# One table of single steps for the start, the weights and each pair of groups

## The chip, the cores and the metric

The kernel runs on one core of one Trainium2 chip. Its time is device microseconds of one execution. Three executions of the kernel before took 2050.55, 2051.13 and 2052.91 us, median 2051.13. The execution that was profiled took 2051.95 us, and its span, from the first instruction to the last, is 2050.2 us. Differences are stated against the median.

## The reference

Keys and values are one tensor: `kv` is averaged over 4 x 4 pixels and multiplied by `w_sr`. Every row of `q` attends to the 768 pooled keys of its batch. A maxout layer with three weight matrices and an output projection follows.

```python
kv_pool = kv.reshape(B, H // r, r, W // r, r, C).mean(axis=(2, 4))   # r = 4
kv_flat = kv_pool.reshape(B, -1, C) @ w_sr                           # 768 keys a batch
k = v = kv_flat
s = scale * (q @ k.transpose(0, 2, 1))
s = s - s.max(-1, keepdims=True)
a = np.exp(s)
a /= a.sum(-1, keepdims=True) + 1e-09
attn_out = a @ v
# then, for x = attn_out as rows of 128 columns
h = np.maximum(np.maximum(x @ w1, x @ w2), x @ w3)                   # 768 columns
return (h @ w_out).astype(np.float32)
```

There are 4 batches of 12288 queries with 128 columns. `q`, `kv` and `w_sr` come as 4-byte numbers, the four layer weights as 8-byte ones.

## The kernel before

The queries are cut into 96 groups of 512, 24 to a batch; a group has four tiles of 128 queries, and the hidden layer of a group six steps of 128 hidden columns. Nearly every operand is kept as two 2-byte halves, a high part and the rest, and a product is three matmuls: high by high, high by low, low by high. The steps of one group have one-letter names in the order tables:

- `S` (`scores`): six matmuls of 384 columns for one tile, into a PSUM tile of two banks; there are two such tiles. `m` (`soft_max`) takes the row maximum on DVE and makes the bias `nb`; `e` (`soft_exp`) is the exponential on ACT with its sum; `c` (`soft_hi`) casts to 2 bytes on ACT; `l` (`soft_lo`) subtracts on POOL and starts the DMA transpose into `aT` on SP's queue.
- `X` (`attend`): half of the attention's product for a group, nine matmuls of 512 columns into the one PSUM tile `ps_x`. `xh` (ACT) and `xl` (DVE) split the result.
- `H` (`hidden`): six matmuls into two PSUM tiles `ps_h`, for w2 − w1 and w3 − w1. `R` (ACT) is a relu of the first, `M` (DVE) a maximum with the second, `C` (ACT) the cast, `L` (POOL) the difference. The next `H` uses the same two PSUM tiles, so it needs `R` and `M` of this one.
- `O` (`project`): three matmuls into `ps_o`; the sixth of a group adds three for x times w1·w_out. `P` (DVE and a DMA transpose), `G` (DVE) and `T` (DVE, a store) turn, merge and scale the output.
- `qd`, `qc`, `qp`, `qh`, `ql`: load 1024 queries, multiply by column factors (POOL), take the size of each row (DVE maximum), split (ACT, DVE) and transpose by DMA.
- `k` (`keys_step`): pooling of the next batch's keys, twelve tiles of 512 KB, with adds on DVE and a few matmuls.

Every instruction on these engines is issued through `InOrder` (line 103 of the profile, a helper, which is why nearly all rows have one line): each engine works through its own instructions in program order. So a table's order is the order of each engine, and an instruction that waits holds back what stands behind it on its engine. SP's queue issues all DMAs in the same way, and a load waits until a buffer of its pool is free (`kv_piece` has 13, shared by key tiles and raw weights; `aT` 2; `q_sb` 2).

The order of the work has four sources. The first batch's keys and the first six tiles' softmax are written out by hand. The weights are a list `todo` of small steps, of which `more(n)` issues the next n at chosen places: `made` lists what one half of a weight matrix needs (clamp, shift, low bits, sign), `halves` and `splits` what follows. From then on `ORDER`, twelve rows for the twelve steps of two groups, is run 48 times by two nested loops; in it a token drains everything that waits for it. Exceptions for the first two groups (`FIRST`, `LEFT`, `ATTEND`, `OUTS`) and the last (`OUTS`, the lines after the loops) are coded separately. The key tiles of the next batch are loaded in `keys_step`, two a group in the groups 1 to 6 of a batch:

```python
if f in (1, 4) and 1 <= r <= 6:
    m = 2 * (r - 1) + f // 4
    n.load(m // R, m % R)
```

The raw 8-byte weights are turned into 4-byte numbers by integer steps on their two words (`Weights64`): the high word is cleared of its sign, clamped, shifted by three, given three bits of the low word and the sign. Then `rest` subtracts w1, `top` and `size_d` find a power of two for the scale, and `split_hi` and `split_lo` make the halves. `product_w1` computes w1·w_out.

At the end `last_project` computes the last group's output with queries as rows. It multiplies with both halves of the weights at once (256 columns), into separate columns of `ps_o` and `ps_x`, so that `last_finish` copies the low columns out on ACT and adds them on DVE before it scales.

Of the kernel before, what the change touches and what calls it, by code (L numbers as in the profile page):

```python
# [20 lines left out]
def kernel(  # L21
# [34 lines left out]
    R = 4  # L56
# [66 lines left out]
    def times(t, src, by, by2=None):  # L123
# [9 lines left out]
    col = const.tile([C, 1], F32, name="col")  # L133
    d_top = const.tile([P, 2, 4], F32, name="d_top")
# [15 lines left out]
    FIRST = (1, 1, 1, 1, 0, 1, 1, 1, 1, 2, 0, 1)  # L150
    LEFT = (12, 12, 12, 12, 12)
    LO_ON_DVE, HI_ON_DVE, HL_ON_DVE = ((), (6, 8), ())
    OUT_AT, OUT_ON = (1, 8), ("dve", "dve")
    ATTEND = {0: (4, 4), 1: (4, 4)}
    LATE = (1,)
    W_LOW, W_HIGH = 2.0 ** -15 * 1.125, 122879.9921875
    HB_ = 5
    ORDER = (
# [12 lines left out]
    )  # L171
    OUTS = {2: (), 3: (), 4: (0, 1, 2)}

    def sr_weights():
# [11 lines left out]
        times(col, ps[:, :1], 1.0)  # L186

# [16 lines left out]
    class Weights64:  # L204
# [7 lines left out]
        def __init__(self, n, w, h, hi, lo, wide=False):  # L212
            self.n, self.h, self.wide, self.w = n, h, wide, w
            self.lay = (lambda t: t.rearrange("p (t c) -> p t c", c=C)) if wide else lambda t: t
            self.hi, self.lo = hi, lo
# [16 lines left out]
        def shift(self):  # L232
            dve.tensor_scalar(
                out=self.e.bitcast(I32), in0=self.e.bitcast(I32), scalar1=3, scalar2=0x3FFFFFF8,
                op0=ALU.logical_shift_left, op1=ALU.bitwise_and,
            )
# [7 lines left out]
        def sign(self):  # L244
            dve.scalar_tensor_tensor(
                out=self.e.bitcast(I32), in0=self.r1, scalar=-0x40000000, in1=self.e.bitcast(I32),
# [6 lines left out]
        def rest(self, on=pool):  # L253
            on.tensor_tensor(out=self.e, in0=self.e, in1=W[0, self.h].e, op=ALU.subtract)
# [14 lines left out]
    def size_d(h):  # L269
        top = d_top[:, h]  # L270
        dve.tensor_reduce(out=top[:, 3:4], in_=top[:, :3], axis=AX.X, op=ALU.max)
        times(top[:, 3:4], top[:, 3:4], col)
        W["ps"] = spare(True)
        mm(out=W["ps"][:, :1], lhsT=ones, rhs=top[:, 3:4], start=True, stop=True)

    def sized_d(h):
        pow2(d_size[h], W.pop("ps")[:, :1], SMALL, LARGE)
# [46 lines left out]
    class Keys:  # L324


        def __init__(self, b):
# [3 lines left out]
            self.acc = {}  # L331
# [3 lines left out]
            self.top = tiny.tile([1, 1], F32, name="pool_top", bufs=2)  # L335
# [24 lines left out]
        def fold(self, s, i, n):  # L360

            view = self.pieces[s, i].rearrange("p (u j c) -> p u j c", u=KU, c=C)
            dve.tensor_tensor(out=view[:, :, :n], in0=view[:, :, :n], in1=view[:, :, n:2 * n], op=ALU.add)

        def gather(self, s, i, n, first, last):
# [4 lines left out]
            for u in range(KU):  # L370
# [13 lines left out]
        def gathered_size(self):  # L384
            self.turn_tops(True)
            self.tops()
            self.size(True)
            self.sized()

        def gathered_project(self, s):  # L390
            if s == 0:
                self.kps = (ps_x.tile([P, G], F32, name="ps_x"), ps_o.tile([P, NJ, C], F32, name="ps_o"))
            out = self.kps[1].rearrange("p j c -> p (j c)") if s == KS - 1 else self.kps[0][:, s * PW:]
# [5 lines left out]
        def gathered_hi(self, n):  # L399
            ps, ks = ((self.kps[0], slice(0, G)), (self.kps[1].rearrange("p j c -> p (j c)")[:, :PW], slice(G, NK)))[n]  # L400
            act.mul(out=self.k_hi[:, ks], in_=ps, mul=self.up)

        def gathered_lo(self, n):
            ps, ks = ((self.kps[0], slice(0, G)), (self.kps[1].rearrange("p j c -> p (j c)")[:, :PW], slice(G, NK)))[n]
# [26 lines left out]
        def turn_tops(self, first=False):  # L431
            self.tops_ps = spare(first)
            dve.tensor_reduce(out=self.m[:, KS:KS + 1], in_=self.m[:, :KS], axis=AX.X, op=ALU.max)
            mm(out=self.tops_ps[:1, :P], lhsT=self.m[:, KS:KS + 1], rhs=ident, start=True, stop=True)

        def tops(self):
            dve.tensor_reduce(out=self.top, in_=self.tops_ps[:1, :P], axis=AX.X, op=ALU.max)

        def size(self, first=False):
            self.size_ps = spare(first)  # L440
# [698 lines left out]
```

## Time and profile before

| | us |
|---|---|
| median of three runs | 2051.13 |
| the profiled execution's own time | 2051.95 |
| its span | 2050.2 |
| PE busy | 1981.4 (97%) |
| DVE busy | 1505.8 (73%) |
| ACT busy | 1453.6 (71%) |
| POOL busy | 1414.8 (69%) |
| mean granted TensorE clock | 0.988 |

Matmuls are pipelined, and their ends are modelled: a matmul of 512 columns is listed with 380 ns, though the next starts before that, so PE's busy time counts a small gap between two of them as busy. Where PE is dense, the distance between the starts is its real step. A stretch's busy time says more than that of the whole span, since the start and the end have other limits than the middle.

### The profile page before, as it was taken

What the parts mean: (1) busy time and instruction counts of PE and PEld (TensorE: products, weight loads), DVE (VectorE), ACT (ScalarE), POOL (GpSimd) and SP (SyncE); (2) the same over time, 40 slices, a digit from 0 to 9 for tenths busy, and PEclk for the clock granted to TensorE, in tenths of its full rate; (3) what the DMA queues carried; (4) which work ended last, traced back from release to release, by engine and by line L of the source; (5) the groups of instructions that cost most, each with busy time, mean ns of one, the idle gap of its engine ahead of it and who ended that gap; (6) DMA issues with size and microseconds to landing.
All of it is one profiled execution on the core that took longest, in us unless ns stands there. A gap on an engine that the chain in (4) does not pass through costs nothing.

```text
span 2050.2 us, 29146 instructions
## 1 busy us (share of the span) xinstructions
PE 1981.4 (97%) x9797; PEld 965.8 (47%) x9797; DVE 1505.8 (73%) x2471; ACT 1453.6 (71%) x2529; POOL 1414.8 (69%) x1068
## 2 busy tenths in 40 slices
PE   5599999999999999999999999999999999999998
PEld 4344444444444444444444444444444444444444
DVE  5758887777777887777777788677776777777775
ACT  3367777777777777777777777677777777777774
POOL 3357776777776677677777777777777777777764
PEclk8699999999999999999999999999999999999999
DMA  8268866767668866675667787666766665667662
GB/s 250 54 137 179 170 139 114 141 131 138 124 126 187 190 132 126 130 145 119 129 139 163 163 173 137 131 127 128 139 132 133 129 139 121 132 131 139 122 120 67
DMA packets 839960, 283.30 MB, mean 138 GB/s; under 512 B 813441, under 2 KB 814593, under 8 KB 839809
## 3 DMA queue, kind: packets, MB, share of 16 engines
q1 hardware_dynamic: 839808, 281.43, 67.2%
q8 instruction: 77, 1.26, 0.2%
q14 instruction: 75, 0.61, 0.1%
HBM read 53.54 MB, written 25.17 MB: 38 GB/s over the span
## 4 chain that ended last, share of the span: by engine, by line
PE 81%; DVE 7%; ACT 4%; DMA 4%; POOL 2%; issue 2%; SPq 0%; DVEq 0%; ACTq 0%; POOLq 0%
PE ps_h L103 31%; PE ps_o L103 18%; PE ps_x L103 17%; PE ps_s L103 15%; DMA aT<-ahl 3%; DVE h L103 1%; ACT ahl L103 1%; POOL ahl L103 1%; DVE w_e L103 1%; DVE q_row L103 1%; ACT a L103 1%; DVE mx L103 1%; ACT hh L103 1%; ACT xh L103 1%; DVE rs L103 1%
## 5 line engine op out<-in xcount | busy, mean ns | idle before, releaser
L103 POOL TENSOR_TENSOR ahl<-a,ahl 128x768 f16<-128x768 f32 x384 | 628.9, 1648 | 307.8 <-issue 188.1
L103 POOL TENSOR_TENSOR hl<-h,hh 128x512 f16<-128x512 f32 x575 | 670.4, 1176 | 191.8 <-ACT hh L103 191.4
L103 DVE SCALAR_TENSOR_TENSOR h<-ps_h,h 128x512 f32<-128x512 f32 x575 | 396.5, 690 | 185.8 <-ACT h L103 92.5
L103 ACT ACTIVATE h<-ps_h 128x512 f32<-128x512 f32 x575 | 341.7, 594 | 244.0 <-PE ps_h L103 240.5
L103 ACT CAST hh<-h 128x512 f16<-128x512 f32 x577 | 349.8, 615 | 170.1 <-DVE h L103 170.0
L103 DVE TENSOR_REDUCE mx<-ps_s 128x1 f32<-128x768 f32 x384 | 366.3, 954 | 108.6 <-PE ps_s L103 107.8
L103 PE MATMUL ps_h<-xh,d_hi 128*128 128x512 f16 x1150 | 437.3, 380 | 5.1 <-DVE h L103 2.7
L103 PE MATMUL ps_h<-xl,d_hi 128*128 128x512 f16 x1150 | 437.2, 380 | 2.9 <-DVE xl L103 2.9
L103 PE MATMUL ps_h<-xh,d_lo 128*128 128x512 f16 x1150 | 437.0, 380 | 0.0
L103 ACT ACTIVATE a<-ps_s,nb,q_sc 128x768 f32<-128x768 f32 x384 | 378.3, 987 | 66.5 <-DVE nb L103 60.4
L103 PE MATMUL ps_x<-aT,v_hi 128*128 128x512 f16 (+1 forms) x1188 | 376.4, 375 | 18.5 <-DMA aT<-ahl 16.7
L103 PE MATMUL ps_s<-k_hi,qT 128*128 128x384 f16 x1536 | 379.0, 329 | 10.6 <-ACT a L103 9.2
L103 PEld LDWEIGHTS <-d_hi 128*128 128x128 f16 x2308 | 226.3, 98 | 260.6 <-issue 6.5
L103 PE MATMUL ps_o<-hh,wo 128*128 128x512 f16 x1140 | 339.1, 379 | 0.0
L103 PEld LDWEIGHTS <-qT 128*128 128x128 f16 x2304 | 227.0, 99 | 203.6 <-issue 17.1
L103 ACT CAST ahl<-a 128x768 f16<-128x768 f32 x382 | 312.5, 832 | 4.5
L103 PEld LDWEIGHTS <-wo 128*128 128x128 f16 x1710 | 167.3, 98 | 191.9 <-issue 0.3
L103 PE MATMUL ps_s<-k_lo,qT 128*128 128x384 f16 x768 | 252.6, 329 | 0.0
L103 PE MATMUL ps_x<-aT,v_lo 128*128 128x512 f16 (+1 forms) x594 | 221.9, 375 | 0.0
L103 PE MATMUL ps_o<-hl,wo 128*128 128x512 f16 x570 | 216.1, 379 | 0.0
L103 POOL TENSOR_TENSOR q_sb<-q_sb,col_row 128x512 f32<-128x512 f32 x96 | 125.2, 1305 | 106.6 <-DMA q_sb<-in_q_dram 96.6
L103 PEld LDWEIGHTS <-v_hi 128*128 128x128 f16 x1188 | 116.5, 99 | 155.4 <-issue 13.1
(141 smaller groups left out, 1416.3 us busy)
## 6 DMA issues: line engine op xcount, KB each, us to landing
kv_piece<-in_kv_dram SPq DMA_DIRECT2D x48, 512.0 KB, 4.8
q_sb<-in_q_dram SPq DMA_DIRECT2D x48, 512.0 KB, 4.4
out_dram<-o_sb SPq DMA_DIRECT2D x95, 256.0 KB, 2.2
aT<-ahl SPq DMA_TRANSPOSE x384, 3.9
kv_piece<-in_moe_w_dram SPq DMA_DIRECT2D x6, 384.0 KB, 4.7
qT<-q_hl SPq DMA_TRANSPOSE x96, 3.4
o_turned<-o_planes SPq DMA_TRANSPOSE x95, 3.1
kv_piece<-in_moe_w_out_dram SPq DMA_DIRECT2D x2, 384.0 KB, 6.8
```

Source lines behind the costliest of these rows:

```text
L103: return lambda **kw: tc.keep_in_program_order(op(**kw))
```

## The change

`ORDER`, the `todo` list, the hand-written start and the exceptions are replaced by three tables of single steps. `START` holds the first batch's keys, the weights, groups 0 and 1 and the first steps of the next ones. `STEADY` holds one pair of groups and is run 45 times. `END` holds the rest. A token issues exactly one step, the next of its kind; with "!" it is issued on another engine (`c!`, `L!`, `l!`, `qc!`: DVE; `qp!`: ACT; `fold…!`: POOL; `wm…!`, `wr…!`: DVE).

With it come:

- Raw weights are loaded ahead of most of the first batch's keys, and the weights' steps stand between the keys' ones.
- A weight half's absolute value and clamp are replaced by one multiplication with 2^−112, on ACT or DVE (`scale`); the shift and sign constants follow.
- `col` is multiplied into the ones of `size_d`'s matmul; the keys' size needs one matmul in place of two, since the first now gives its result on all partitions.
- `q_peak` with "!" sums absolute values on ACT where it took the maximum on DVE.
- Later batches' keys are loaded one tile a group over twelve groups; their sums stand at the groups in `KEYS_AT`.
- `last_project` makes three products of 128 columns into one region of PSUM, and `last_finish` scales it straight from there.

```diff
-    FIRST = (1, 1, 1, 1, 0, 1, 1, 1, 1, 2, 0, 1)
-    LEFT = (12, 12, 12, 12, 12)
...
+    W_DOWN = 2.0 ** -112
+    KEYS_AT = ((3, 5, 6, 7), (8, 9, 10, 11), (12, 13, 14, 15))
...
-    ORDER = (
-        "H e C l L m k R c M X O S qc",
-        "H C R O G c L m M S l e qc k X",
...
+    START = (
+        "wd.2.0 wd.2.1 wm.2.0! ws.2.0 wl.2.0 wd.0.1 wm.0.1 wd.0.0 sr wm.0.0! qd qc! qc! wd.1.0",
+        "ws.0.1 wl.0.1 wn.0.1 wm.1.0 ws.1.0 wl.1.0 kv.2.0 wm.2.1! ws.2.1 kv.1.2 qp! kv.1.0 wn.1.0 kv.1.1",
+        "wl.2.1 ws.0.0 add.1.1.2 kv.2.1 add.2.0.1 wl.0.0 wn.0.0 wn.2.1 qd qc! qc wd.1.1 wm.1.1 kv.1.3",
+        "wr.2.1 qh wn.2.0 wt.0.1 gat.1.0.4 gat.1.1.4 end.1.3.4 wr.1.0! kv.0.0 ws.1.1 wl.1.1 kv.0.3 wr.2.0 fold.2.0.2!",
+        "gat.0.0.4 kv.0.1 kv.0.2 wn.1.1 gat.2.0.2 qh kv.2.2 fold.2.2.2! kv.2.3 wd.3.1 ql wt.1.0 add.0.2.3 qp!",
+        "wt.2.0 qd wt.0.0 gathered_peak.1 gat.0.1.4 end.0.2.4 fold.2.3.2.1! gathered_peak.0 wm.3.1 gat.2.2.2 ql gat.2.3.4.0 end.2.3.2.1 ws.3.1",
+        "wd.3.0 wr.1.1 dsize.0 gathered.1 wt.1.1 gathered_peak.2 turn_tops tops gathered.0 gathered_project.0 gathered.2 kd sized gathered_project.1",
+        "gathered_hi.0 qe gathered_lo.0 gathered_project.2 gathered_hi.1 value.0 gathered_lo.1 S qh ql qh S m e",
+        "turn_w1.0 m e value.1 c! l c wt.2.1 S m e S dsize.1 wl.3.1",
+        "c m e dsized.0 wh.2.0 S qe turn_w1.1 m l l c! e c",
+        "S m e l l X c S l X ql m e S",
+        "X wo.2.0 dsized.1 m wh.1.0 S wh.1.1 ka X S e qc wo.1.0 m",
+        "xh xl wm.3.0! c! c ws.3.0 H R M wh.2.1 H R e wo.2.1",
+        "M wo.1.1 H R M H R C S m M C H e",
...
+    )
+    STEADY = (
+        "H qd kd ka qc c R M qc L m O qp! m",
+        "e C L H R l kd M X X ka xh xl H",
+        "R l e O C M H R G M S L C L",
+        "m T C L c l O c H R M e O O",
+        "l H S c P O R M qh H C R qh ka",
+        "m G M ka e ka L! C S H c ql C R",
+        "X M L S O X m m e c! H O l l",
+        "l xh xl R M ka H S S e R L O M",
+        "H C c C C qe L m R m e e L l",
+        "M L O O P H R S S M C c T ql",
+        "C O L",
+    )
+    END = (
...
+        "C M last_hidden G T O O C L O last_project.3 L last_project.4 last_project.5",
+        "last_finish",
+    )
...
-        def clamp(self, on=dve):
+        def scale(self, on=None):
             self.e = wprep.tile([P, HALF_F], F32, name="w_e")
-            if on is pool:
-                act.activation(out=self.e, in_=self.r1.bitcast(F32), func=AF.Abs)
+            if on:
+                times(self.e, self.r1.bitcast(F32), W_DOWN)
             else:
-                dve.tensor_scalar(
-                    out=self.e.bitcast(I32), in0=self.r1, scalar1=0x7FFFFFFF, scalar2=None, op0=ALU.bitwise_and
+                act.mul(out=self.e, in_=self.r1.bitcast(F32), mul=W_DOWN)
...
-            on.tensor_scalar(
-                out=self.e, in0=self.e, scalar1=W_LOW, scalar2=W_HIGH, op0=ALU.max, op1=ALU.min
-            )
...
-        times(top[:, 3:4], top[:, 3:4], col)
-        W["ps"] = spare(True)
-        mm(out=W["ps"][:, :1], lhsT=ones, rhs=top[:, 3:4], start=True, stop=True)
+        W["ps", h] = spare(True)
+        mm(out=W["ps", h][:, :1], lhsT=col_ones, rhs=top[:, 3:4], start=True, stop=True)
...
-            mm(out=self.tops_ps[:1, :P], lhsT=self.m[:, KS:KS + 1], rhs=ident, start=True, stop=True)
+            mm(
+                out=self.tops_ps[:, :P], lhsT=self.m[:, KS:KS + 1].to_broadcast([P, P]), rhs=ident,
+                start=True, stop=True,
+            )
...
-        def size(self, first=False):
-            self.size_ps = spare(first)
-            mm(out=self.size_ps[:, :1], lhsT=ones[:1], rhs=self.top, start=True, stop=True)
...
+        if summed:
+            act.activation(
+                out=qp.tile([P, SJ * C], F16, name="q_abs", bufs=1), in_=st["q"][s].rearrange("p j c -> p (j c)"),
+                func=AF.Abs, accum_out=row,
+            )
...
-                for i, h_ in enumerate((hh, hl)):
+                for i, (h_, s) in enumerate(((hh, 1), (hh, 0), (hl, 0))):
                     for j in range(n):
                         mm(
-                            out=o[:, j], lhsT=h_[:, (off + j) * P:(off + j + 1) * P], rhs=w,
+                            out=o[:, j], lhsT=h_[:, (off + j) * P:(off + j + 1) * P], rhs=w[:, s],
...
-            act.copy(out=lo, in_=o[:, :, 1])
-            dve.tensor_tensor(out=osb[:, half], in0=o[:, :, 0], in1=lo, op=ALU.add)
             dve.scalar_tensor_tensor(
-                out=osb[:, half], in0=osb[:, half], scalar=w_down,
+                out=osb[:, half], in0=o, scalar=w_down,
...
+    def keys_load(b, r):
+        if r == 1:
+            KT[b] = Keys(b)
+        if r <= KS * R:
+            KT[b].load(*divmod(r - 1, R))
...
+    KT[0] = Keys(0)
+    run(START)
+    for _ in range(NG // 2 - 3):
+        run(STEADY)
+    run(END)
```

In the tables `kv.s.i` loads a key tile, `add`, `fold`, `gat`, `end` and `gathered…` sum the first batch's keys and collect them through PE, and `w` steps are those of the weights: `wd` load, `wm` scale, `ws` shift, `wl` low bits, `wn` sign, `wr` rest, `wt` top, `wh` and `wo` the two halves; the numbers are the matrix (0 to 2 are w1 to w3, 3 is w_out) and its half.

More of the change, by code (lines that the diff above doesn't have):

```diff
@@ L951, in step @@
-    def step(token, g, f):
-        n = g * NFT + f
-        if token == "H":
-            hidden(g, f)
-            to_relu.append((g, f))
+    tiles = [(g, j) for g in range(NG) for j in range(NJ)]
+    products = [(0, j) for j in range(NJ)] + [(g, part) for g in range(1, NG) for part in range(2)]
+    steps = [(g, f) for g in range(NG) for f in range(NFT)]
+    halves_q, eights_q = (list(range(n)) for n in (NG, NG // 2))
+    next_keys = [(b, r) for b in range(1, B) for r in range(1, GPB + 1)]
@@ L1112, with run @@
+    def run(rows):
+        for row in rows:
+            for token in row.split():
+                start(token)
+    KT[0] = Keys(0)
[3 more added lines that the diff above has]
+    run(END)
+    assert not any(v for t, v in todo.items() if t[0] != "k")
 _INS = ["q", "kv", "w_sr", "moe_w1", "moe_w2", "moe_w3", "moe_w_out"]
```

501 lines of the change are left out of this document (174 added, 327 removed), and 33 rows, old and new, of tables (END, ORDER, START).

## The prediction

> **What bounds the kernel now.** I read the windows of busy time first, then the PE groups of the first 150 us, the chain of waits there, and the timelines of one steady stretch and of the end. The windows show, for each stretch, busy time and instruction count of PE, PEld, DVE, ACT and POOL, then PE's granted clock, the DMA share and GB/s.
>
> ```profile
> 25.00:50.00 25.00, 11.04 (x42) 5.10 (x42) 15.09 (x33) 11.79 (x20) 12.57 (x9) 0.75 0.67 181
> 50.00:75.00 25.00, 12.32 (x92) 8.14 (x92) 19.03 (x37) 6.09 (x11) 11.77 (x10) 0.70 0.36 69
> 75.00:100.00 25.00, 15.99 (x57) 7.95 (x57) 20.34 (x47) 11.32 (x22) 7.15 (x5) 0.66 0.14 26
> 100.00:150.00 50.00, 44.54 (x216) 21.53 (x217) 28.25 (x46) 29.86 (x54) 29.18 (x23) 0.97 0.71 146
> ...
> 400.00:600.00 200.00, 200.00 (x987) 96.34 (x985) 145.36 (x234) 148.66 (x260) 144.19 (x110) 1.00 0.67 132
> 600.00:800.00 200.00, 196.34 (x968) 94.45 (x967) 160.97 (x257) 146.95 (x256) 144.98 (x109) 1.00 0.78 161
> ...
> 200.00:2025.00 1825.00, 1810.85 (x8910) 871.30 (x8908) 1356.14 (x2199) 1344.02 (x2335) 1304.99 (x983) 1.00 0.69 138
> 2025.00:2050.20 25.20, 19.01 (x119) 11.12 (x117) 14.78 (x26) 9.84 (x19) 8.03 (x7) 0.96 0.14 43
> ```
>
> From 200 us on PE is the bound and nearly full: 1825 − 1810.85 = 14.15 us idle in 1825. No order of the other engines' work can win more than that there. The first 100 us are another kernel: between 25 and 100 us PE is busy 39.4 of 75 us, at a granted clock of 0.66 to 0.75. So the question is when PE gets full.
>
> To price that, I need PE's steps at full rate:
>
> ```profile
> 1499.99 0.49 PE L103 MATMUL ps_s<-k_hi,qT 128*128 128x384 f16 x2
> 1500.96 0.59 PE L103 MATMUL ps_o<-hh,wo 128*128 128x512 f16 x2
> 1501.61 0.38 PE L103 MATMUL ps_h<-xh,d_hi 128*128 128x512 f16 x1
> 1502.91 0.59 PE L103 MATMUL ps_o<-hh,wo 128*128 128x512 f16 x2
> 1503.55 0.38 PE L103 MATMUL ps_x<-aT,v_hi 128*128 128x512 f16 x1
> 1505.50 0.38 PE L103 MATMUL ps_h<-xh,d_hi 128*128 128x512 f16 x1
> ```
>
> From start to start: a score tile S 0.97 us, a projection O 0.65, a hidden step H 1.30, half an attention X 1.95.
>
> And what PE has done by 150 us:
>
> ```profile
> L103 PE MATMUL ps_s<-k_hi,qT 128*128 128x384 f16 x78 | 23.2, 386 | 10.6 <-ACT a L103 9.2 <-ACT k_hi L103 1.4
> L103 PE MATMUL ps_x<-aT,v_hi 128*128 128x128 f16 (+1 forms) x78 | 16.1, 317 | 6.8 <-DMA aT<-ahl 6.8
> L103 PE MATMUL ps_h<-xh,d_hi 128*128 128x512 f16 x32 | 13.4, 420 | 5.1 <-DVE h L103 2.7 <-ACT xh L103 2.4
> L103 PE MATMUL ps_o<-hh,wo 128*128 128x512 f16 x26 | 7.7, 379 | 0.0
> L103 PE MATMUL ps_h<-d_top,ones 128*128 128x1 f32 x4 | 1.1, 355 | 9.4 <-DVE d_top L103 9.4
> ```
>
> Four k_hi matmuls make an S, two xh,d_hi matmuls an H, two hh,wo matmuls an O: 19.5 S, 16 H, 13 O. Of the attention's 78, group 0 has 48 narrow ones and two and a half groups the other 30.
>
> **The change, part by part.**
>
> *The START table.* It ends after 20 S, 15 H, 13 O and the attention of groups 0, 1 and 2. Before, 150 us bring half an S less (+0.5 us), one H and half a group's attention more (−1.3, −1.95): the same point is reached at about 150 − 2.75 = 147.3 us. What follows is the same PE work. So the table's worth is 147.3 minus the time T at which the new table ends. I build T in three pieces.
>
> Piece one, to the first score. Before, it starts here:
>
> ```profile
> 30.46 0.80 PE L103 MATMUL ps_s<-k_hi,qT 128*128 128x384 f16 x2 [1.36 <-ACT k_hi L103]
> 59.67 0.38 PE L103 MATMUL ps_h<-xh,d_hi 128*128 128x512 f16 x1 [2.39 <-ACT xh L103]
> ...
> 16.00:20.00 4.00, 2.83 (x25) 2.83 (x26) 3.48 (x4) 1.09 (x2) 0.00 (x0) 1.00 1.03 410
> ...
> 25.51 1.50 POOL w_e L103
> ```
>
> Now six weight halves and a second q load stand ahead of the last key tile on SP's queue: a weight half is 128 × 768 words of 4 bytes, 0.393 MB, a q load 128 × 1024, 0.524 MB, so 6 × 0.393 + 0.524 = 2.9 MB more, at 410 GB/s 7 us. Before, key loads and one q load (6.8 MB) end near 20 us; now near 27. SP's 14th piece also waits until DVE has finished the first weight half, since there are 13 buffers; the keys queued behind it wait too. I count 16 us of DVE steps ahead of that, plus the wait for an early key tile: about 20 us, when the loads ahead are just done, so nothing is added. From last key to first score the old kernel takes 10.5 us. In them the chain of waits holds a weight clamp on POOL (1.50 us, the last row) with 1.7 us of weight steps around it, and a second tiny matmul for the keys' size, 0.6 us; all this goes or moves. I take 10.5 − 3.8 = 6.7 us: first score near 34, 3.5 us later than before.
>
> Piece two, to the first H: 59.67 − 30.46 = 29.2 us before. On the chain of waits there (start, length, what) stand, among softmax steps:
>
> ```profile
> 39.53 2.42 POOL w_e L103 x2
> ...
> 41.98 1.79 DVE w_e L103
> ...
> 51.73 1.32 DVE w_e L103
> 53.07 1.68 DVE w_e L103
> ```
>
> These are weight steps, 7.2 us, and shorter ones with the sizes some 2.6 us more. In the new table those of w1, w2 and w3 are nearly all issued while the keys load. On the other side, the table issues nine softmax tiles ahead of the first H, the old code six:
>
> ```profile
> L103 DVE TENSOR_REDUCE mx<-ps_s 128x1 f32<-128x768 f32 x384 | 366.3, 954 | 108.6 <-PE ps_s L103 107.8
> L103 DVE TENSOR_SCALAR nb<-mx,q_sc 128x1 f32<-128x1 f32 x384 | 82.2, 214 | 13.7
> L103 DVE TENSOR_SCALAR w_e<-w_e 128x384 f32<-128x384 f32 x5 | 4.3, 852 | 0.2
> ```
>
> Three more are 3.5 us. 29.2 − 9.8 + 3.5 = 22.9: first H near 57.
>
> The new decode itself: the clamp (852 ns, five on DVE) becomes one scaling, four of eight on ACT, the shift and the two steps behind it stay. This saves DVE 3 to 4 us; the place counts for more.
>
> Piece three: from there PE owes 15 H, 11 S, 4 halves of attention, 13 O, twice the extra 0.65 us of a group's last O, and the weight product: 19.5 + 10.7 + 7.8 + 8.5 + 1.3 + 1.4 = 49 us. DVE owes about as much (11 maxima 12.8, 15 h steps at 0.69 = 10.4, the rest of w_out, splits, q, moved casts: some 43), so PE won't be quite dense. I use the share of 100 to 150 us, 44.54 of 50: 49/0.89 = 55. T = 57 + 55 = 112; gain 35 us. Dense PE from 54 on would give T = 103, gain 44; T = 124 (twice the idle, first H at 60) a gain of 23.
>
> *The STEADY table.* PE's matmuls stay the same. Per pair one cast c moves from ACT to DVE, one hl difference from POOL to DVE, and q's row size from DVE (a maximum) to ACT (a sum of Abs). DVE is 73% busy: 1356.14 of 1825 us, so the counts hide in its idle time; the danger is the order, below.
>
> The keys' loads matter more. Two tiles a group fall into six groups of each batch; one tile a group spreads them over twelve. In the windows above, 400 to 600 us has no load burst and no idle PE, while 600 to 800 us has one and 3.66 us idle. Of PE's waits from 200 to 2025 us (total, times, longest), this is the largest:
>
> ```profile
> PE ps_x L103 <- DMA aT<-ahl: 9.0, 9, 1.8
> ```
>
> These 9.0 us can shrink. Against that, PE's order has H, O, H with just one O between, three times per pair. Its second accumulator must be read by the h step before the next H refills it.
>
> ```profile
> L103 DVE SCALAR_TENSOR_TENSOR h<-ps_h,h 128x512 f32<-128x512 f32 x575 | 396.5, 690 | 185.8 <-ACT h L103 92.5
> L103 ACT ACTIVATE h<-ps_h 128x512 f32<-128x512 f32 x575 | 341.7, 594 | 244.0 <-PE ps_h L103 240.5
> ```
>
> From H's start: first half written after some 0.8 us (two steps of 0.22 and a matmul's 0.38), relu till 1.5, h step till 2.3, with 0.1 us for each handing over; the refill comes at 1.30 + 0.65 + 0.65 = 2.6. That leaves 0.3 us, if ACT and DVE are free at once. Bounds: −9 if all transpose waits go; +15 if a third of a microsecond is lost in each of the 45 pairs. I take −3, on the side of the row.
>
> *The end.*
>
> ```profile
> 2041.00 1.11 DVE L103 TENSOR_SCALAR rs<-sm,o_down 128x4 f32<-128x4 f32 x1
> 2043.44 0.74 DVE L103 SCALAR_TENSOR_TENSOR h<-ps_s,h 128x256 f32<-128x256 f32 x2
> 2044.34 0.39 PE L103 MATMUL ps_o<-wo,hh 128*128 128x256 f16 x2 [1.37 <-ACT hh L103]
> 2045.28 0.37 ACT L103 COPY h<-ps_o 128x256 f32<-128x256 f32 x1 [0.67 <-PE ps_o L103]
> 2047.00 0.48 DVE L103 SCALAR_TENSOR_TENSOR o_sb<-o_sb,w_down,rs 128x256 f32<-128x256 f32 x1
> ```
>
> The last h steps wait behind the scaling of older groups on DVE and make PE wait 1.37 us; the new table issues them ahead of it. The low half of the output no longer needs its own PSUM columns, so an ACT copy (0.37) and a DVE sum go: about 1.2 us from PE's end to the last store. Together −2.6; bounds −1.2 (PE still waits) and −3.5.
>
> *Sum.* −35 − 3 − 2.6 = −40.6 against the profiled execution's own 2051.95 us (span 2050.2 us): 2011.4. The median of the runs lies 0.8 below it, so 2010.5.
>
> **The rivals.**
>
> A: the slow clock stays. Its granted mean of 0.70 and 0.66 between 50 and 100 us goes with a PE that is idle a third to half of the time; the first scores above took 0.80 us for a pair of matmuls that takes 0.49 later. If piece three still has such gaps, its 49 us take 49/0.68 = 72, plus 6 us idle: T = 135, gain 12, with the other terms 2033. Against it: DVE's weight work, which opened those gaps, is mostly gone by then. The Trainium skill, "TensorE: Matmul & The Clock Gate", section on the HAM clock gate, says that PE falls to half rate after an idle window of about 3.4 us and comes back after a busy one as long; the slow pair agrees. By that rule piece three would be slow only in its first microseconds, which speaks for T near 112.
>
> B: slower. The cast that moves to DVE. These are the two such casts of the old kernel:
>
> ```profile
> 83.60 0.56 DVE L103 CAST ahl<-a 128x768 f16<-128x768 f32 x1 [0.55 <-ACT a L103]
> 95.56 1.75 DVE L103 CAST ahl<-a 128x768 f16<-128x768 f32 x1 [0.28 <-ACT a L103]
> ```
>
> One takes 0.56 us, the other, beside a POOL at work, 1.75, and POOL is busy 1304.99 of 1825 us. Queued behind it are xl and the h step, for which the next hidden step on PE waits. If those 1.19 us reach PE in every pair, 45 pairs cost 54 us: 2010.5 + 54 = 2064. From 40.6/45 = 0.9 us of new PE wait a pair the change is a loss. Against it: in the row the cast stands two PE steps ahead of xl. The Trainium skill, "GPSIMD Engine Reference", section 8, says that GpSimd shares its SBUF interfaces with VectorE and contends with DVE instructions in a 2-port mode or with two SBUF inputs; the pair of casts agrees, and the moved hl difference, with two SBUF inputs, would be the second such step per pair.
>
> C: the change doesn't do what it says. The weights come early, but first the keys and then the softmax of the first groups hold PE back as long, so T stays near 147 and only the end and the transposes gain: 2051.1 − 5.6 = 2045.5. For it: the 9.2 us PE waited for a<-ps_s in the score rows. Against it: 9.4 us waited for d_top, and the slots of idle DVE under the loads are real.
>
> **How the numbers follow.** The forecast has 0.68, with its own range of 1996 (gain 44, −9, −3.5, rounded up) to 2027 (gain 23, steady even, end −1.2); A 0.12, B 0.11, C 0.09. About 0.2%, 4 us, is what a measurement here tells from no change. Faster are the forecast, A and C but for a small part of it (0.03, the same): 0.86; slower is B: 0.11. The range runs from 1996 to 2037, to include A and leave out B and C.
>
> **What would show it.** First score near 34 us, first H near 57, the table's end (15 H, 20 S, 13 O) near 112; few w_e steps on DVE after the first H; PE idle from 200 us on below 14 us, its waits on aT below 9; no PE wait on hh at the end. Wrong it is if H starts after 65 us, if the granted clock between 60 and 110 us stays below 0.8, or if PE shows h, xl or xh waits in each pair of the steady part.

## The result, and the profile after

The changed kernel takes 2102.45 us (median of four, 2102.15 to 2103.62), the kernel before beside it 2051.61. The ratio is 1.0249, with a 95% interval of 1.0231 to 1.0266: slower by 51 us, where 40 us less was forecast. Unless said otherwise, all times below are medians, and the kernel before lay between 2051.4 and 2053.6 us beside each of them.

First the page of the changed kernel, its line of busy times:

```profile
span 2101.8 us, 29591 instructions
PE 1991.5 (95%) x9825; PEld 962.2 (46%) x9825; DVE 1689.9 (80%) x2517; ACT 1439.9 (69%) x2572; POOL 1428.6 (68%) x1012
```

DVE was busy 1505.8 us before and is busy 184 us longer, with nearly the same steps: the moved ones add 71 us (differences and casts) and take away 57 (the maxima of q). That is the first hint. The windows (busy time of PE, of PEld, which is PE's loading of weights, of DVE, ACT and POOL, then clock, DMA share, GB/s) and two rows of PE's timeline say when the time was lost:

```profile
36.51 0.48 PE L103 MATMUL ps_s<-k_hi,qT 128*128 128x384 f16 x2 [0.44 <-ACT k_hi L103]
56.69 0.38 PE L103 MATMUL ps_h<-xh,d_hi 128*128 128x512 f16 x1
...
25.00:50.00 25.00, 18.65 (x137) 14.20 (x138) 22.22 (x53) 12.93 (x25) 10.33 (x7) 1.00 0.87 201
50.00:107.50 57.50, 56.37 (x324) 29.33 (x323) 45.99 (x84) 43.82 (x79) 40.06 (x29) 1.00 0.63 114
107.50:2060.00 1952.50, 1868.73 (x9061) 888.91 (x9060) 1573.78 (x2303) 1356.84 (x2424) 1352.36 (x952) 0.99 0.66 133
```

The start did what was said of it: first score at 36.5 us (34 predicted), first H at 56.7 (57), PE full from 50 us on at a clock of 1.00. The 25th hidden step starts 40.4 us earlier than before (137.7 against 178.1). From there the lead melts: by the 553rd hidden step it has become a lag of 52.9 us. So 93 us are lost in 44 pairs, 2.1 us in each. In the third window PE is idle 83.8 us; before, from 147.3 to 2010 us, it was 14.5. Two smaller parts make up the rest. Where PE is dense, a matmul's listed end lies 0.16 us behind the start of the next (0.38 against 0.22), so each wait is that much longer than listed, 14 us for the 86 waits more. The lower granted clock that the last section shows takes 10 us.

PE's waits from 200 to 2060 us name the place (total, times, longest):

```profile
PE ps_h L103 <- DVE h L103: 70.4, 85, 2.3
PE ps_x L103 <- DMA aT<-ahl: 4.4, 7, 1.3
PE ps_h L103 <- ACT h L103: 3.1, 4, 1.6
```

The waits for transposes shrank, as forecast. In their place PE waits for M, the maximum h. The next view shows why M is late: DVE groups of the middle, first after (200 to 2060 us), then before (200 to 2010 us); behind the bar are busy time and mean ns of one.

```profile
L103 DVE SCALAR_TENSOR_TENSOR h<-ps_h,h 128x512 f32<-128x512 f32 x522 | 358.6, 687 | 187.9 <-ACT h L103 140.0 <-PE ps_h L103 42.9
L103 DVE SCALAR_TENSOR_TENSOR o_sb<-o_sb,w_down,rs 128x512 f32<-128x512 f32 x87 | 147.2, 1692 | 3.1
L103 DVE SCALAR_TENSOR_TENSOR q_hl<-q_sb,q_up,q_hl 128x512 f16<-128x512 f32 x86 | 131.2, 1525 | 0.0
L103 DVE TENSOR_SCALAR rs<-sm,o_down 128x4 f32<-128x4 f32 x87 | 88.1, 1012 | 0.0
L103 DVE TENSOR_TENSOR kv_piece<-kv_piece 128x512 f32<-128x512 f32 x49 | 66.9, 1382 | 0.0
```

```profile
L103 DVE SCALAR_TENSOR_TENSOR o_sb<-o_sb,w_down,rs 128x512 f32<-128x512 f32 x89 | 94.8, 1065 | 3.2
L103 DVE TENSOR_SCALAR rs<-sm,o_down 128x4 f32<-128x4 f32 x89 | 65.7, 738 | 0.0
L103 DVE SCALAR_TENSOR_TENSOR q_hl<-q_sb,q_up,q_hl 128x512 f16<-128x512 f32 x88 | 65.5, 744 | 0.0
L103 DVE TENSOR_TENSOR kv_piece<-kv_piece 128x512 f32<-128x512 f32 x48 | 37.5, 782 | 0.0
```

The same instructions on the same tiles take up to twice as long: 1525 against 744 ns for the low half of q. And one pair in which keys are summed (rows of DVE, of POOL, and PE's wait):

```profile
1403.44 0.69 DVE L103 SCALAR_TENSOR_TENSOR h<-ps_h,h 128x512 f32<-128x512 f32 x1 [0.17 <-ACT h L103]
1404.05 1.07 DVE L103 TENSOR_SCALAR rs<-sm,o_down 128x4 f32<-128x4 f32 x1
1405.15 0.18 DVE L103 RECIPROCAL rs<-rs 128x4 f32<-128x4 f32 x1
1405.36 1.50 DVE L103 SCALAR_TENSOR_TENSOR o_sb<-o_sb,w_down,rs 128x512 f32<-128x512 f32 x1
1406.79 1.75 DVE L103 SCALAR_TENSOR_TENSOR q_hl<-q_sb,q_up,q_hl 128x512 f16<-128x512 f32 x1
1408.46 1.64 DVE L103 TENSOR_TENSOR kv_piece<-kv_piece 128x512 f32<-128x512 f32 x1
1410.02 0.68 DVE L103 SCALAR_TENSOR_TENSOR h<-ps_h,h 128x512 f32<-128x512 f32 x1
...
1403.93 1.16 POOL L103 TENSOR_TENSOR hl<-h,hh 128x512 f16<-128x512 f32 x1 [2.01 <-ACT hh L103]
1405.05 2.94 POOL L103 TENSOR_TENSOR q_sb<-q_sb,col_row 128x512 f32<-128x512 f32 x2
1407.95 1.60 POOL L103 TENSOR_TENSOR hl<-h,hh 128x512 f16<-128x512 f32 x1
...
1403.14 0.49 PE L103 MATMUL ps_s<-k_hi,qT 128*128 128x384 f16 x2
1410.75 0.38 PE L103 MATMUL ps_h<-xh,d_hi 128*128 128x512 f16 x1 [2.27 <-DVE h L103]
```

This is a loop of two engines. DVE needs 6.6 us from the end of one maximum (1404.1, 1.0 us behind the hidden step that it reads) to the end of the next (1410.7); between the two lie T (rs, reciprocal, o_sb), `ql` (q_hl) and `ka` (kv_piece), 6.1 us by their lengths, while POOL works almost without a pause. PE, from the end of the hidden step that the first maximum reads (1403.1), has two scores, a projection, a hidden step, a projection and half a hidden step to do, 5.2 us, and then stands still until the second maximum is written. Where no keys are summed the wait is 0.71 us; a second spot, where only T stands ahead of M, costs 0.35 to 0.57 us in each pair.

From here on there are two theories, which may both hold. **Order**: T, `ql` and `ka` stand together in one loop. **POOL**: they are slow because POOL works beside them. The rivals are the prediction's B (the cast moved to DVE) and the other moves between engines.

### The profile page after: what moved, and what is told of

The parts are those of the page before. It is cut to its first block, busy times and chain, and to the rows that moved or that the text cites. A ratio compares the mean times of both kernels' runs of the same rounds, so it can differ in the third digit from the quotient of the medians.

```text
span 2101.8 us, 29591 instructions
## 1 busy us (share of the span) xinstructions
PE 1991.5 (95%) x9825; PEld 962.2 (46%) x9825; DVE 1689.9 (80%) x2517; ACT 1439.9 (69%) x2572; POOL 1428.6 (68%) x1012
## 4 chain that ended last, share of the span: by engine, by line
PE 60%; DVE 20%; issue 7%; ACT 5%; DMA 4%; POOL 3%; SPq 0%; DVEq 0%; ACTq 0%
PE ps_h L103 23%; PE ps_x L103 16%; PE ps_s L103 11%; PE ps_o L103 11%; DVE h L103 5%; DVE rs L103 4%; DVE o_sb L103 4%; DMA aT<-ahl 3%; DVE mx L103 2%; ACT h L103 2%; DVE q_hl L103 2%; POOL ahl L103 2%; ACT a L103 1%; DVE kv_piece L103 1%; POOL hl L103 1%
## 5 line engine op out<-in xcount | busy, mean ns | idle before, releaser
L103 POOL TENSOR_TENSOR hl<-h,hh 128x512 f16<-128x512 f32 x525 | 632.5, 1214 | 569.2 <-ACT hh L103 466.1
L103 POOL TENSOR_TENSOR ahl<-a,ahl 128x768 f16<-128x768 f32 x382 | 666.5, 1760 | 77.8 <-DVE ahl L103 65.7
L103 PE MATMUL ps_s<-k_hi,qT 128*128 128x384 f16 x1536 | 374.6, 326 | 3.3 <-ACT a L103 2.7
L103 PE MATMUL ps_x<-aT,v_hi 128*128 128x512 f16 (+1 forms) x1188 | 371.8, 377 | 4.8 <-DMA aT<-ahl 4.6
L103 ACT CAST ahl<-a 128x768 f16<-128x768 f32 x332 | 272.0, 831 | 24.4 <-DMA aT<-ahl 23.0
L103 PEld LDWEIGHTS <-d_lo 128*128 128x128 f16 x1154 | 112.7, 98 | 232.5 <-issue 115.0
```

The source lines that it names most:

```text
L103: return lambda **kw: tc.keep_in_program_order(op(**kw))
```

## The experiments

### Which of the two, and is it the cast?

The diffs here and below show the steady table; rows of START and END that have to follow at the seams are left out. e1_order moves `ql` and `ka` behind M; e2_noqc leaves out POOL's multiplications of q, so its output is another; e3_cast takes the cast back.

```diff
 e1_order
-"M L O O P H R S S M C c T ql",   "H qd kd ka qc c R M qc L m O qp! m",
+"M L O O P H R S S M C c T",      "H qd kd qc c R M ql ka qc L m O qp! m",
 e2_noqc
-"H qd kd ka qc c R M qc L m O qp! m",
+"H qd kd ka c R M L m O qp! m",
 e3_cast
-"X M L S O X m m e c! H O l l",
+"X M L S O X m m e c H O l l",
```

> The changed kernel with one change in the steady table: the low half of q (ql) and the key sum (ka) are issued on VectorE behind M (the maximum that frees PE's second accumulator) and no longer ahead of it; engines, instructions and PE's order stay. Theory 1, late maximum: M is late because the steps ahead of it on VectorE are too many for the one projection that lies between two hidden steps; with 1.75 and 1.64 us taken from ahead of it the 2.27 us wait (keyed pairs) and the 0.71 us wait (others) go, 52 us, and with them the 10 us that the lower granted clock behind some of them costs: 2102 - 62 = about 2040. The waits of 0.35 to 0.56 us fifteen us later stay. Rival, the moved cast (the prediction's B): the order here plays no part, 2102, at most 4 us off. Rival, the key loads one tile a group: 2102.

> The changed kernel without POOL's two multiplications of q by the column factors (qc) in the steady table; they are left out, so the queries of these groups stay unscaled and the output is another. The order of everything else stays. Theory 2, VectorE is slowed while POOL works: o_sb and q_hl, 1.69 and 1.75 us beside POOL and 0.75 alone, fall toward 0.75 where qc ran beside them, M comes 1.7 us earlier, the long wait falls to about 0.5 us, the 0.71 us wait goes: 2102 - 59 = about 2043, with the count and the order of VectorE's steps untouched. If only the number of steps ahead of M counts, the time stays within 5 us of 2102.

> The changed kernel with the one softmax cast per pair (c with the mark) back on ScalarE in the steady table. Prediction's rival B: 1.19 us a pair go, 2102 - 54 = 2048. Theories 1 and 2: the cast took 0.57 us on VectorE and stands behind no hidden step that PE waits for: 2102, 4 us up or down.

Measured: e1_order 2077.39 us (ratio 1.012, 1.010 to 1.014), e2_noqc 2041.82 (0.9946, 0.9931 to 0.9961), e3_cast 2107.32 (1.027, 1.0251 to 1.029). Three DVE groups of e2_noqc, from 200 to 1950 us, and PE's waits in e1_order from 200 to 2030 us:

```profile
L103 DVE SCALAR_TENSOR_TENSOR q_hl<-q_sb,q_up,q_hl 128x512 f16<-128x512 f32 x84 | 87.5, 1042 | 0.0
L103 DVE SCALAR_TENSOR_TENSOR o_sb<-o_sb,w_down,rs 128x512 f32<-128x512 f32 x85 | 144.2, 1696 | 3.0
L103 DVE TENSOR_TENSOR kv_piece<-kv_piece 128x512 f32<-128x512 f32 x49 | 53.5, 1108 | 0.0
```

```profile
PE ps_x L103 <- DMA aT<-ahl: 19.8, 25, 2.2
PE ps_h L103 <- ACT h L103: 19.2, 32, 1.8
PE ps_h L103 <- DVE h L103: 5.3, 16, 1.3
```

POOL is confirmed, and the time was met to 1 us: without its two steps, order and count of all others unchanged, 61 us come back. The terms were partly others than expected. q_hl fell, from 1525 to 1042 ns, and so did the key sum, from 1382 to 1108; o_sb, which was to fall too, did not (1692 and 1696), since POOL's `L` and `l` still run beside it. In one pair with keys, from 1357.09 us on, q_hl and the key sum take 0.74 and 0.68 us, and DVE needs 4.6 us from maximum to maximum, less than PE's 5.2. Not all of the gain need be the slowing of DVE, since POOL also has 2.9 us less of its own per pair. Order came to less than half of what was expected: the wait for M is gone (70 to 5 us), but 39 us of waits for transposes and relus stand in its place. Rival B falls for this kernel: without the moved cast it is no faster.

### Moving more, or moving POOL's steps

e5_all also puts both T behind the next M. e4_qclate moves the multiplications instead, e6_qcdve gives them to DVE, e7_both is e1_order with e4_qclate.

```diff
 e5_all
-"m T C L c l O c H R M e O O",  "M L O O P H R S S M C c T ql",  "H qd kd ka qc c R M qc L m O qp! m",
+"m C L c l O c H R M T e O O",  "M L O O P H R S S M C c",       "H qd kd qc c R M T ql ka qc L m O qp! m",
 e4_qclate
-"H qd kd ka qc c R M qc L m O qp! m",  "e C L H R l kd ...",        "R l e O C M H R G M ...",
+"H qd kd ka c R M L m O m",            "e C L qc qc H R l kd ...",  "R l e O C qp! M H R G M ...",
 e6_qcdve
-"H qd kd ka qc c R M qc L m O qp! m",
+"H qd kd ka c R M qc! qc! L m O qp! m",
```

> As e1_order, and both scalings of the output (T: three VectorE steps, 2.8 to 3 us beside POOL) are issued behind the next M as well. Theory 1: all waits of PE for the maximum go, also those of 0.35 to 0.56 us, 2102 - 90 = about 2012, which is what the start table alone would leave: 2051 - 40. If POOL's work beside VectorE finds another step to slow that PE waits for, 2030 to 2060.

> The changed kernel with POOL's two multiplications of q (qc) behind the low half L of the next row, so that they run after M and not beside o_sb and q_hl; ScalarE's sum of q moves behind them. Nothing is left out. Theory 2: o_sb and q_hl ahead of M fall toward 0.75 us, the waits go as without qc: 2040 to 2060, more than 2043 as far as the two multiplications now slow a step that PE waits for later. If only the number of steps counts: 2102.

> The changed kernel with the two multiplications of q on VectorE, behind M, in place of POOL: 2.9 us a pair less on POOL, two steps of about 0.7 us more on VectorE. Theory 2: 2043 to 2060, VectorE with more instructions and less busy time than in the changed kernel. If VectorE's load as such is the bound (it is busy 80% of the time), the time rises above 2102.

> e1_order and e4_qclate together: the low half of q and the key sum behind M, and POOL's multiplications of q later. If late M is the only thing that the two cure, it is cured twice, and what is left is the second wait of about 0.35 us a pair and what e1 showed in its place (waits for the attention's transposes and for ScalarE's relu, 39 us together): 2040 to 2065. If the two gains add: 2102 - 25 - 60 = 2017.

Measured: e5_all 2169.22 (1.0569, 1.0554 to 1.0585), e4_qclate 2297.04 (1.1185, 1.117 to 1.1201), e6_qcdve 2064.97 (1.0057, 1.0043 to 1.007), e7_both 2330.38 (1.1343, 1.1326 to 1.136). Only e6_qcdve came out near its range. Its DVE has 90 instructions more than the changed kernel's and yet 15 us less busy time (1674.9 against 1689.9), as expected if POOL slows them. PE's largest wait in e5_all (200 to 2030 us), and one DVE row with PE's largest wait in e4_qclate (200 to 1950 us):

```profile
PE ps_o L103 <- DVE o_planes L103: 60.5, 41, 2.2
```

```profile
1727.85 0.15 DVE L103 TENSOR_SCALAR q_row<-q_row 128x1 int32<-128x1 int32 x1 [4.55 <-ACT q_abs L103]
...
PE ps_h L103 <- ACT h L103: 150.7, 37, 4.5
```

In e5_all, P, the copy that frees ps_o, now stands behind T, and PE waits for it 1.5 us a pair. In e4_qclate the place in question was cured (q_hl before that M takes 0.74 us), but POOL's `l` came later, ScalarE's exponential waited for it, and behind that came the sum of q and the relu `R`, for which PE waits longest; on DVE the sum's small steps, ahead of the next M, waited 4.55 us. Each cure moved the wait to what was queued behind the step that moved.

### The loop itself

e8_gap puts a score tile on PE into the tight spot, from ahead in the same loop. e11_into takes a tile from outside the loop, with its softmax behind it. e12_early_t moves one word: T ahead of the first of the two maxima.

```diff
 e8_gap
-"M L O O P H R S S M C c T ql",  "H qd kd ka qc c R M qc L m O qp! m",
+"M L O O P H R S M C c T ql",    "H qd kd ka qc c R M qc L m S O qp! m",
 e11_into
-"l xh xl R M ka H S S e ...",  "... R m e e L l",  "H ... qc c R M qc L m O qp! m",    "e C L H R l kd M X X ...",
+"l xh xl R M ka H S e ...",    "... R e L l",      "H ... qc R M qc L m S O qp! m",  "e e c C L H R l kd M m X X ...",
 e12_early_t
-"M L O O P H R S S M C c T ql",
+"M L O O P H R S S T M C c ql",
```

> The changed kernel with one score tile (S) moved on PE from the pair's next-to-last row to the place between two hidden steps that had one projection between them; the order of the other engines stays. The maximum M gets 0.97 us more before PE needs it. Prediction's tight spot (0.3 us of slack): the 2.27 us wait falls to 1.3, the 0.71 us wait goes, and with the shorter waits the lower clock: 2102 - 18 - 17 - 10 = about 2057. If the score tile that comes later makes the softmax and with it the transposes late, part of it comes back as waits on aT: up to 2080. If M is late whatever PE does meanwhile: 2102.

> The changed kernel with one score tile of a pair moved from ahead of both hidden steps (row 8 of the steady table) to between the two (row 1); its maximum, exponential and cast follow it. Loop theory: M is late by VectorE's steps between two maxima (rs, reciprocal, o_sb, q_hl, the key sum, h: 6.8 us in keyed pairs) less PE's work between the same two hidden steps; a tile moved within the loop (e8_gap) changed nothing, one moved into it gives 0.97 us: the 2.27 us wait becomes 1.3, the 0.71 us wait goes, 2102 - 45 = about 2057, less what the added maximum takes back on VectorE (it stands behind M). If M is late for another reason: 2102.

> The changed kernel with the second scaling of a pair (T: rs, reciprocal, o_sb, 2.75 us) ahead of the previous maximum on VectorE in place of behind it. Loop theory: the loop that ends in the 2.27 us wait loses 2.75 us, its wait goes, 2102 - 62 = about 2040, if the maximum that now stands behind T has room. If it has none, the wait only moves one hidden step ahead: 2090 to 2110.

Measured: e8_gap 2101.69 (1.0241, 1.0227 to 1.0255), e11_into 2343.92 (1.1425, 1.1407 to 1.1443), e12_early_t 2034.4 (0.9918, 0.9901 to 0.9934). PE's waits in e12_early_t and the largest in e11_into, 200 to 1950 us:

```profile
PE ps_h L103 <- ACT h L103: 9.8, 12, 1.6
PE ps_h L103 <- DVE h L103: 9.6, 27, 0.4
PE ps_x L103 <- DMA aT<-ahl: 4.9, 9, 0.9
```

```profile
PE ps_s L103 <- ACT a L103: 181.2, 37, 5.8
```

In e8_gap the wait stayed at 2.27 us, since the tile was in the loop already: the spot between two H is not what decides, the sum around the loop is. e12_early_t gives the loop 2.75 us on DVE and gains 68 us, within 6 us of what was expected; this one word makes the changed kernel 0.8% faster than the one before. It does not test order alone, since T also got shorter: at its new place rs and o_sb take 0.28 and 0.75 us in 42 pairs, where they took 1.07 and 1.50 in the example above. e11_into tests nothing cleanly: the wait for M shrank to 0.3 us, but the tile's exponential came so late on ScalarE that scores found no free PSUM tile.

### Order or engines? The old order between the new start and end

h1_old_steady and e9_engines differ in the steady order, and a few seam steps, alone. The others add the moves to h1_old_steady or take one part alone. Of k1_keys only the loads are shown; its sums move as in the change.

```diff
 h1_old_steady: STEADY
-"H qd kd ka qc c R M qc L m O qp! m",
-...
+"H C L L R m M l l S e O c",    "H C m l R M O e X",
+"H C xh xl R c M L L S O qp qe ka",  "H C m l R M e ka c L O S",
+"H C G R l L O m M kd X e",     "H P ka C R T M O S c",
+"H L C qh R m M l O S e ql c",  "H L m qh R l M e X O C C ql",
+"H xh L L xl c R M O S ka qd",  "H C l L m ka R M O S qc",
+"H C R O G L m M e e qc kd X",  "H P C T c c R O M S ka",
 e9_engines: the changed STEADY with c!, L!, qp!
-c!  L!  qp!
+c   L   qp
 e10_marks: h1_old_steady with all three of m1, m2, m3
 m1_cast
-"H P ka C R T M O S c"
+"H P ka C R T M O S c!"
 m2_sum
-"H C xh xl R c M L L S O qp qe ka"
+"H C xh xl R c M L L S O qp! qe ka"
 m3_diff
-"H C G R l L O m M kd X e"
+"H C G R l L! O m M kd X e"
 m4_diff_later
-"H C m l R M e ka c L O S"
+"H C m l R M e ka c L! O S"
 k1_keys: the kernel before
-        if f in (1, 4) and 1 <= r <= 6:
-            m = 2 * (r - 1) + f // 4
-            n.load(m // R, m % R)
+        if f == 1 and 1 <= r <= KS * R:
+            n.load(*divmod(r - 1, R))
```

> The start table and the end table of the changed kernel with the old order of a pair of groups between them: the twelve rows of ORDER are written out as single steps, begun at the row that follows the start table's end, with the casts on ScalarE, the differences on POOL and q's row size on VectorE as in the kernel before; keys still one tile a group. A few steps at the seams (one score tile less, half an attention, q's factors and one scaling more at the end of the start table) make the two fit. If the whole loss lies in the steady table's order, this is the kernel before minus the start's 40 us and the end's 1: about 2010 (2004 to 2018). If the start table leaves something behind that costs later, or the key loads do, it is above 2030. If the prediction's forecast of the two tables was right but for the steady order, its own 2010.5.

> The changed kernel with all three moved steps of the steady table back on their old engines: the cast on ScalarE, the difference hl on POOL, q's row size as a maximum on VectorE. Theory 1 and 2 (the order of the steps, with POOL beside VectorE): 2102, 10 us up or down. If the moves between engines are the loss: below 2060.

> h1_old_steady with the changed kernel's three moves between engines in each pair: one cast and one difference on VectorE, the sum of q on ScalarE. Theory: in an order that leaves room ahead of each maximum they cost nothing, 2000, 4 us up or down. If the moves are the loss, 45 pairs at 1 to 2 us: 2045 to 2090.

> The kernel before with one part of the change alone: later batches' key tiles are loaded one a group over twelve groups, and their sums stand at the groups that the change gives them, two steps a group. The prediction's transposes: 9 us of waits for aT under the loads shrink to a third, 2051 - 3 to 6 = 2045 to 2048; h1_old_steady gained 5 us over the kernel before between its start and its end, which this would account for. If that gain has another source: 2051.

> h1_old_steady with one cast of the softmax a pair on VectorE, nothing else. Prediction's B: 1.19 us a pair, 2000 + 54. The cast took 0.55 us, never beside POOL, in e10_marks; if it costs its own length at most: 2000 to 2025, if it stands in idle time 2000.

> h1_old_steady with q's row size as a sum on ScalarE, nothing else: 2000, 5 us up or down. Then the third move, the difference hl on VectorE (1.75 us there beside POOL, 0.68 alone, ahead of the copy that frees ps_o), carries most of e10_marks' 70 us.

> h1_old_steady with one difference hl a pair on VectorE at e10_marks' place, where VectorE waits 1.35 us for hh on ScalarE and then takes 1.77 us beside POOL, with a maximum and the copy that frees ps_o behind it. It carries the rest of the 70 us: 2000 + 55 to 65 = 2055 to 2065. If the three moves only cost together: below 2020.

> h1_old_steady with one difference hl a pair on VectorE, but the one of the row before, behind M, where hh is done and 0.8 us of idle VectorE follow. If the place decides: 2000 to 2010. If VectorE has no room for 0.7 us anywhere, or is slowed beside POOL there too: 2030 to 2065.

| | us | ratio, 95% interval |
|---|---|---|
| h1_old_steady | 2000.51 | 0.9745, 0.9731 to 0.9759 |
| e9_engines | 2104.57 | 1.0256, 1.0242 to 1.027 |
| e10_marks | 2070.51 | 1.0088, 1.0072 to 1.0103 |
| m1_cast | 2007.45 | 0.9782, 0.9765 to 0.9798 |
| m2_sum | 2000.57 | 0.9753, 0.9738 to 0.9767 |
| m3_diff | 2094.99 | 1.021, 1.0193 to 1.0227 |
| m4_diff_later | 2007.62 | 0.9784, 0.977 to 0.9799 |
| k1_keys | 2040.14 | 0.9944, 0.9931 to 0.9956 |

h1_old_steady beats the kernel before by 2.55% and the changed one by 102 us. Its windows and its low half of q, then the hl differences on DVE in m3_diff and in m4_diff_later, then PE's waits for M in m3_diff and in e10_marks (all 200 to 1950 us):

```profile
200.00:1000.00 800.00, 795.37 (x3919) 383.72 (x3918) 601.78 (x996) 591.11 (x1031) 574.61 (x432) 1.00 0.71 143
1000.00:1950.00 950.00, 948.39 (x4673) 456.97 (x4672) 701.73 (x1143) 704.52 (x1226) 681.18 (x514) 1.00 0.68 136
L103 DVE SCALAR_TENSOR_TENSOR q_hl<-q_sb,q_up,q_hl 128x512 f16<-128x512 f32 x86 | 63.9, 743 | 0.0
```

```profile
L103 DVE TENSOR_TENSOR hl<-h,hh 128x512 f16<-128x512 f32 x41 | 73.4, 1789 | 34.4 <-ACT hh L103 34.4
```

```profile
L103 DVE TENSOR_TENSOR hl<-h,hh 128x512 f16<-128x512 f32 x44 | 30.0, 682 | 0.0
```

```profile
PE ps_h L103 <- DVE h L103: 43.8, 52, 2.1
...
PE ps_h L103 <- DVE h L103: 13.5, 25, 0.8
```

e9_engines and h1_old_steady have the same steps on the same engines; their orders are 104 us apart. So the steady table's order is the loss, all of it. The theory of POOL is part of this, not its rival: the order decides which DVE steps fall beside POOL. In the old order q_hl takes 743 ns, in e9_engines, with the same steps on POOL, 1305. But "the moves cost nothing in an order with room" fell too: three of them cost 70 us in the old order. The cast costs 7, the sum nothing, the difference alone 94, more than with the other two beside it. One row earlier the same difference costs 7. At m3_diff's place it waits for its operand (34.4 us in all), then takes 1789 ns beside POOL; at m4_diff_later's place 682 ns and no wait. One step a pair, one row apart: 87 us. PE waits for M here too, 43.8 us in m3_diff and 13.5 in e10_marks; why the other two moves shorten this wait was not found out.

## Why the prediction was wrong

**The start** was right: about 40 us against 35, in its bounds. First score and first H hide two errors that cancelled: piece one took 2.5 us more than forecast, piece two 2.7 less (20.2 against 22.9), which is luck. The share of idle PE that it took for the third piece (0.89) was too cautious, since PE was busy 56.37 of 57.5 us from 50 us on.

**Rival A** did not come: the clock is 1.00 in both early windows. **C** fell with the start.

**The steady table, −3 with bounds −9 to +15, is the step that failed.** Its sentence "DVE is 73% busy: 1356.14 of 1825 us, so the counts hide in its idle time; the danger is the order, below" looked in the right place (in that stretch it is 74%; 73% is the share of the whole span), and "H, O, H with just one O between" named the wait that came. But it priced the order on PE alone: 0.3 us of slack "if ACT and DVE are free at once". The row order "… c T ql" and "H qd kd ka … M" was there to be read: T, `ql` and `ka` between two maxima, 2.6 us by their lengths with POOL at rest (0.27 + 0.18 + 0.75 + 0.74 + 0.68, the table at the end), 6.1 us beside POOL. The two durations of one cast, 0.56 and 1.75, had been quoted, and the price of 1.19 us was put on the cast only, not on the other steps of DVE that read two SBUF tiles. What was missing is a sum around each loop: DVE's steps from one M to the next, at their lengths beside POOL, against PE's work between the same two H. With alone lengths M would have been in time (3.5 us earlier, the wait 2.27), so both causes are needed: e2_noqc took away part of POOL's work and left the order, e12_early_t moved T and so shortened it too, and each gave 61 to 68 us. The prediction's own sign of being wrong, waits for h in each pair, is what came.

**B** had the right resource, sharing between DVE and POOL, and the wrong instruction. The cast took 566 ns in the changed kernel and never ran beside POOL for its whole length; undone, it gained nothing, and in the old order it costs 7 us, not 54. The difference hl, which B named in passing, could cost 94.

**The keys' loads**: the right sign, but too small: k1_keys alone gains 11 us. PE's waits for aT over the whole span, first in the kernel before, then in k1_keys:

```profile
PE ps_x L103 <- DMA aT<-ahl: 16.7, 13, 4.7
```

```profile
PE ps_x L103 <- DMA aT<-ahl: 9.1, 7, 4.7
```

That is 7.6 us of the 11. Two waits that the profile lists as issue, 1.8 us together, are gone as well, and eight waits fewer, each 0.16 us longer than listed, make another 1.3.

**The end** gained 0.7 us and not 2.6: from the start of the last H to the end of the span it takes 12.2 us (2089.57 to 2101.8) against 12.95. PE's own part became 0.3 us shorter, the time from PE's last matmul to the end of the span 0.4. A wait for hl (0.45 us) and a scaling of an older group ahead of the last two steps on DVE stand in the way; that they account for all of the rest is not shown.

The 51 us that h1_old_steady gains split into about 11 for the keys, 0.7 for the end and the remaining 39 for the start, if they add. Only the first was measured by itself, but in its trace the 13th and the 25th hidden step start 38.9 and 37.5 us earlier than before, which agrees with the last.

## What to carry to other kernels

Before an order is called safe, sum each in-order engine's steps between two of its hand-overs to the bound engine, at the lengths they have beside the engine that slows them, and compare with the bound engine's work between the same two: an average busy share of 73% says nothing about it. Moving a step to cure a wait moves everything queued behind it; of the seven reorderings of the changed table (e1, e4, e5, e7, e8, e11, e12) only the last, which took work out of the loop and put it where DVE had room, gave what was expected.

## What the runs showed of the hardware

**DVE beside POOL.** DVE instructions of the changed kernel from 200 us on, sorted by the share of their length in which a POOL instruction ran (median us; count):

| DVE instruction | no POOL | POOL over 90% |
|---|---|---|
| q_hl, two SBUF tiles | 0.74 (18) | 1.75 (63) |
| o_sb, two SBUF operands | 0.75 (3) | 1.69 (86) |
| copy o_sb<-o_turned | 0.74 (51) | 0.99 (10) |
| rs, 4 elements | 0.27 (1) | 1.07 (90) |
| key sum kv_piece, two SBUF tiles | 0.68 (19) | 2.18 (14) |
| reciprocal, 4 elements | 0.18 (4) | 0.18 (88) |
| h, one input from PSUM | 0.68 (113) | 0.69 (330) |
| mx, reduction of PSUM | 0.94 (115) | 0.95 (204) |

This is a wait for POOL's instruction, not a shared speed: q_hl of 1406.79 ends at 1408.54, 0.55 us behind the end of POOL's multiplications (1407.99), and needs 0.74 us alone. So it is with all 64 slowed q_hl, all 88 slowed o_sb and all 27 slowed key sums, whatever POOL runs: each ends 0.54 to 0.55 us behind the end of a POOL instruction (rs 0.02 to 0.03, the copy 0.60 to 0.62). The wait goes the other way too. In these rows of e12_early_t o_sb starts first and takes its 0.75 us, and POOL's hl takes 1.55 us, where the one ahead of it took 1.15:

```profile
1306.39 1.15 POOL L103 TENSOR_TENSOR hl<-h,hh 128x512 f16<-128x512 f32 x1
...
1309.33 0.75 DVE L103 SCALAR_TENSOR_TENSOR o_sb<-o_sb,w_down,rs 128x512 f32<-128x512 f32 x1
1309.55 1.55 POOL L103 TENSOR_TENSOR hl<-h,hh 128x512 f16<-128x512 f32 x1 [2.01 <-ACT hh L103]
```

The Trainium skill, "SBUF — State Buffer", section "SBUF: two separate sides", says the same: a VectorE instruction in a 2-port mode or with two SBUF inputs and a GpSimd one hold one port pair in turn, each for its whole length. Short steps pay as well: rs, with four elements a row, loses 0.80 us, nearly as much as o_sb (0.94); the reciprocal loses nothing.

**The granted clock falls after a wait of 2.27 us.** Windows of the changed kernel around such a wait, which ends at 1365.64:

```profile
1360.00:1364.00 4.00, 3.38 (x16) 1.45 (x15) 3.93 (x5) 2.40 (x4) 4.00 (x3) 1.00 0.35 99
1364.00:1368.00 4.00, 2.35 (x6) 0.84 (x6) 3.90 (x8) 1.33 (x4) 0.44 (x1) 0.71 0.74 216
1368.00:1372.00 4.00, 4.00 (x17) 1.70 (x16) 3.01 (x4) 0.83 (x2) 3.59 (x3) 0.87 0.30 116
```

The two windows below full clock lose 1.7 us of it. The clock fell in this way after six of the fifteen waits of 2.27 us; summed over 4 us windows from 104 to 2060 us, that costs 10 us. It did not follow the other nine; what sets the six apart is not shown. The Trainium skill, "TensorE: Matmul & The Clock Gate", section "What's actually happening", puts the fall behind an idle window of about 3.4 us, which is free-running; here a listed wait of 2.27 us was enough six times, and the measurement decides.
